# Column sums of w_out by sixteen column-tiled TensorE products in place of GpSimd additions

## The chip, the cores and the metric

The kernel runs on one core of a Trainium2 chip. A core has TensorE (PE in the profile, with its weight loads PEld), VectorE (DVE), ScalarE (ACT), GpSimd (POOL) and SyncE (SP), a working memory SBUF and an accumulation memory PSUM that TensorE writes. The metric is the device time of one execution in microseconds (us).

## What is computed

A block-sorted attention followed by a two-layer network on its output. With B, H, S, D = 4, 8, 768, 64 and eight blocks of 96 rows:

```python
# P: sort_net after five rounds of exp, row and column normalisation (8x8 per head)
k_sorted = einsum('bhij,bhjcd->bhicd', P, k_blocks)
v_sorted = einsum('bhij,bhjcd->bhicd', P, v_blocks)
attn = softmax(scale * q_block @ k_sorted_block.T) @ v_sorted_block
x = attn.transpose(0, 2, 1, 3).reshape(3072, 512)
r = maximum(x @ w_in, 0)          # w_in 512 x 2048
out = (s * r * r + b) @ w_out     # w_out 2048 x 512, s and b scalars
```

The kernel uses that (s r² + b) @ w_out is s (r² @ w_out) plus b times the column sums of w_out. The column sums are one row of 512 numbers, needed once.

## The kernel before

The 3072 tokens are worked on in eight half batches t = 0 to 7 of 384 tokens (four blocks of 96). t // 2 is the batch. For each half batch s_piece (L358) makes scores of a pair of heads and ScalarE's exponential (L361), p_piece (L385 to L390) multiplies by the sorted values and normalises into X[t], and t_piece (L413, for t = 0 and 1) turns X[t] on TensorE into tr and copies it to XT[t] (xt, L228). Later half batches are turned by DMA (x_turn).

ffn1(t) is the first layer: eight steps, each of eight products hps (L442) for 256 of the 2048 inner columns, a Relu on ScalarE (rt, L446), a square on VectorE (gt, L447), and then a call of slot(), which lets one piece of other work into the engines' queues. A Queue spreads its list of pieces evenly over the slots. ffn2(t) is the second layer: three groups of 128 tokens, each sixteen products ops (L468) over the inner columns, with a slot after every four.

The order of work on every engine is the order in which the program is written. Around the change it is: ffn1(0) in two halves (192 tokens each), whose slots hold attention pieces and, in the second half, V1(0) to V1(3) and the turning of half batch 1; then V1(4) and V1(5); then ffn1(1); then ffn2(0) and ffn2(1) with the queue qu, which begins with pieces of batch 1's queries and keys.

V1(i) is v_piece1 (L312 and after): two products tv (L319) of 64 columns of the array each, 512 wide, a cast vn (L228) on VectorE, and two writes dv (L325) to DRAM on SP's queue. When all six are written, v_read(1) on SP's queue (L344) reads the values of batch 1 back in another order; p_piece(2, ...) is the first to use them. build_pd2 (L526) makes the block matrix pd2 for batches 2 and 3, used first by v_piece2 (V2, L333).

The column sums csum are made on GpSimd: after a small copy (gate, L582), which waits for the last piece of X[1], csums(0, 8) adds the first eight of the sixteen 128x512 pieces of w_out (wo_at, tiles wo, loaded at L154) element by element and csums(8, NF) the rest, so csum holds 128 rows of partial sums. bias_piece (L510), in the sixth piece of qu, multiplies by onesf, a 128x128 matrix of ones, which adds up the 128 rows and spreads the sum over all of them, and then by b. GpSimd's queue also issues the loads of q, k, v and the weights: load_v(*brows(3)) stands between the two halves of the additions, load_k for batches 2 and 3 and load_q(2) behind the second, ahead of bias_piece in the same piece.

PSUM tiles come from two pools, psa (three buffers) and psb (two); a new tile of a pool waits until the one whose buffer it takes has been read. tv, ops and pe (of build_pd2) are in psb; hps, tr of a whole half batch and the key pieces of sixteen products are in psa.

Of the kernel before, what the change touches and what calls it, by code (L numbers as in the profile page):

```python
# [9 lines left out]
FP = mybir.dt.float32  # L10
BF = mybir.dt.bfloat16
AF = mybir.ActivationFunctionType
ALU = mybir.AluOpType
# [5 lines left out]
def kernel(  # L19
# [12 lines left out]
    nc = tc.nc  # L32
# [6 lines left out]
    d_model = H * D  # L39
    d_ff = moe_w_in.shape[1]  # L40
    NF = d_ff // 128
    HB = NB // 2
# [10 lines left out]
    const = ctx.enter_context(tc.tile_pool(name="const", bufs=1))  # L53
    sk = ctx.enter_context(tc.tile_pool(name="sk", bufs=1))
# [12 lines left out]
    psb = ctx.enter_context(tc.tile_pool(name="psb", bufs=2, space=bass.MemoryType.PSUM))  # L67
# [22 lines left out]
    def load_v(rows, prow):  # L90
        nc.gpsimd.dma_start(out=vb[prow, 0:BLK, :], in_=vraw[rows])

    def brows(b):
        return slice(b * 64, (b + 1) * 64), slice((b % 2) * 64, (b % 2) * 64 + 64)
# [12 lines left out]
    def new_vs(b):  # L107
        VS[b] = vsp.tile([BLK, 64, VW], BF, tag="vs", name=f"vs{b}")
        nc.vector.memset(VS[b][:, :, D:VW], 1.0)
# [33 lines left out]
    for c0 in range(0, d_ff, FCH):  # L143
        w = const.tile([128, NHP, FCH], BF, name=f"wi{c0}")
        nc.gpsimd.dma_start(
            out=w, in_=moe_w_in.rearrange("(hp p) f -> p hp f", p=128)[:, :, c0:c0 + FCH])
        wis.append(w)
    onesf = const.tile([128, 128], FP)
    nc.gpsimd.memset(onesf, 1.0)

    load_v(*brows(1))
    for f0 in range(0, NF, FW):
        w = const.tile([128, FW, d_model], BF, name=f"wo{f0}")
        nc.gpsimd.dma_start(  # L154
            out=w, in_=moe_w_out.rearrange("(f p) n -> p f n", p=128)[:, f0:f0 + FW, :])
# [4 lines left out]
    def wi_at(hp, f):  # L160
        return wis[f * 128 // FCH][:, hp, f * 128 % FCH:f * 128 % FCH + 128]

    def wo_at(f):
        return wos[f // FW][:, f % FW, :]
# [9 lines left out]
    def zero_pad(r0):  # L174
# [8 lines left out]
                            op=ALU.subtract)  # L183
    between = [lambda: zero_pad(BLK), lambda: zero_pad(BLK + 16), lambda: None,
               lambda: None, lambda: None]
    for it in range(5):
# [5 lines left out]
                                op=ALU.mult)  # L192
# [119 lines left out]
    def v_piece1(c0, eng):  # L312

        pr = brows(1)[1]
        ps = psb.tile([128, 8, D], FP, tag="b", name="tv")
        lhsT = pd1[pr].rearrange("p e m i -> p (e m i)")
        hb = BLK // 2
        for hf in range(2):
            nc.tensor.matmul(out=ps[hf * 64:(hf + 1) * 64], lhsT=lhsT,  # L319
                             rhs=vb[pr, hf * hb + c0:hf * hb + c0 + 8, :],  # L320
                             start=True, stop=True)
        vn = vnp.tile([128, 16, D], BF, tag="vn", name="vn")
        evac(vn[:, 0:8, :], ps, eng)
        for hf in range(2):
            nc.sync.dma_start(out=dv[1][:, hf * hb + c0:hf * hb + c0 + 8, :],  # L325
                              in_=vn[hf * 64:(hf + 1) * 64, 0:8, :])
# [12 lines left out]
    def v_read(b, eng):  # L339
        if b > 1:  # L340
            new_vs(b)
        src = dv[1] if b == 1 else dv[2][(b - 2) * 64:(b - 1) * 64]
        for cp in range(2):
            eng.dma_start(out=VS[b][cp * (BLK // 2):(cp + 1) * (BLK // 2), :, 0:D],  # L344
                          in_=src.rearrange("g (c two) d -> two c g d", two=2)[cp])

    XT, AT, X = {}, {}, {}

    def s_piece(t, hp):

        b, half = divmod(t, 2)
        g0 = (b % 2) * 32 + hp * NB + half * HB
        sc = psa.tile([BLK, 2, 512], FP, tag="a", name="sc")
        for n in range(HB):
            for e in range(2):
                pr = slice(e * 64, (e + 1) * 64)
                q0 = (half * HB + n) * BLK
                nc.tensor.matmul(out=sc[:, e, n * BLK:(n + 1) * BLK], lhsT=ks[pr, g0 + n, :],  # L358
                                 rhs=QT[b][pr, hp, q0:q0 + BLK], start=True, stop=True)
        at = atp.tile([BLK, 2, TG], BF, tag="at", name="at")  # L360
        nc.scalar.activation(out=at, in_=sc[:, :, 0:TG], func=AF.Exp, scale=scale)  # L361
        AT[t, hp] = at

    def p_piece(t, hp, n0=0, nn=HB):

        b, half = divmod(t, 2)
        at = AT[t, hp]
        if t not in X:
            X[t] = xp.tile([BLK, HB, d_model], BF, tag="x", name="x")
        x = X[t]  # L370
        atf = at.rearrange("p e t -> p (e t)")
        if nn < HB:
            p1 = psb.tile([128, 512], FP, tag="b", name="pv")
            pv = [p1[:, e * nn * VW:(e + 1) * nn * VW] for e in range(2)]
            pvv = p1[0:BLK, 0:2 * nn * VW].rearrange("p (e n w) -> p e n w", e=2, w=VW)
        else:
            p2 = psa.tile([128, 2, 512], FP, tag="a", name="pv")
            pv = [p2[:, 0], p2[:, 1]]
            pvv = p2[0:BLK, :, 0:nn * VW].rearrange("p e (n w) -> p e n w", w=VW)
        for e in range(2):  # L380
            for n in range(n0, n0 + nn):
                c0 = (e * HB + n) * BLK
                m = 128 if c0 + 128 <= 2 * TG else BLK
                gi = e * 32 + hp * NB + half * HB + n
                nc.tensor.matmul(out=pv[e][0:m, (n - n0) * VW:(n - n0 + 1) * VW],  # L385
                                 lhsT=atf[:, c0:c0 + m],
                                 rhs=VS[b][:, gi, :], start=True, stop=True)
        rec = rtp.tile([BLK, 2, HB], FP, tag="rec", name="rec")
        nc.vector.reciprocal(out=rec[:, :, 0:nn], in_=pvv[:, :, :, D])  # L389
        nc.vector.tensor_tensor(  # L390
            out=x[:, n0:n0 + nn, hp * 128:(hp + 1) * 128].rearrange("p n (e d) -> p e n d", e=2),
            in0=pvv[:, :, :, 0:D],
            in1=rec[:, :, 0:nn].unsqueeze(3).broadcast_to([BLK, 2, nn, D]), op=ALU.mult)
# [29 lines left out]
    def xt_at(t, hp, n0, nn):  # L423
        if t < 2:
            return XT[t][:, hp, n0 * BLK:(n0 + nn) * BLK]
        return XT[t].rearrange("p (n a) t -> p a n t", a=NHP)[:, hp, n0:n0 + nn, :]
# [6 lines left out]
    def ffn1(t, slot=nothing, n0=0, nn=HB):  # L433
        if t not in GT:
            GT[t] = gtp.tile([128, NF, TG], BF, tag="gt", name="gt")
        gt = GT[t]
        c0, nt = n0 * BLK, nn * BLK
        for f0 in range(0, NF, 2):
            hps = psa.tile([128, 2, 512], FP, tag="a", name="hps")
            for f in range(2):  # L440
                for hp in range(NHP):
                    nc.tensor.matmul(out=hps[:, f, 0:nt], lhsT=wi_at(hp, f0 + f),  # L442
                                     rhs=xt_at(t, hp, n0, nn),
                                     start=(hp == 0), stop=(hp == NHP - 1))
            rt = rtp.tile([128, 2, TG], BF, tag="rt", name="rt")
            nc.scalar.activation(out=rt[:, :, 0:nt], in_=hps[:, :, 0:nt], func=AF.Relu)  # L446
            nc.vector.tensor_tensor(out=gt[:, f0:f0 + 2, c0:c0 + nt], in0=rt[:, :, 0:nt],  # L447
                                    in1=rt[:, :, 0:nt], op=ALU.mult)
            slot()
# [113 lines left out]
    def P(t, hp, *r):  # L563
        return lambda: p_piece(t, hp, *r)

    def SC(t, hp):
        return lambda: s_piece(t, hp)

    def V1(i):
        return lambda: v_piece1(i * 8, "v")  # L570

    ffn1(0, Queue([P(0, 0, 2, 2), P(0, 1, 2, 2), P(0, 2, 2, 2), P(0, 3, 2, 2), SC(1, 2),
                   lambda: t_piece(0, "v", 2, 2), SC(1, 3), P(1, 0)], 8), 0, 2)
    ffn1(0, Queue([V1(0), P(1, 1), V1(1), P(1, 2), V1(2), P(1, 3), V1(3),
                   lambda: t_piece(1, "v")], 8), 2, 2)
    V1(4)()
    V1(5)()


    csum = const.tile([128, d_model], FP)  # L580
    gate = sk.tile([1, 1], BF)
    nc.gpsimd.tensor_copy(out=gate, in_=X[1][0:1, HB - 1, d_model - 1:d_model])  # L582

    def csums(f0, f1):
        for f in range(f0, f1):
            if f == 1:
                nc.gpsimd.tensor_tensor(out=csum, in0=wo_at(0), in1=wo_at(1), op=ALU.add)
            elif f > 1:
                nc.gpsimd.tensor_tensor(out=csum, in0=csum, in1=wo_at(f), op=ALU.add)  # L589

    csums(0, 8)
    v_read(1, nc.sync)
    ffn1(1, Queue([nothing] * 4 + [build_pd2] + [nothing] * 3, 8))
    load_v(*brows(3))
    csums(8, NF)

    V2 = [lambda c0=c0: v_piece2(c0, "s") for c0 in range(0, BLK, 16)]
    qu = Queue([lambda: q_piece(1, 0, "s"), lambda: q_piece(1, 2, "v")]
# [67 lines left out]
```

The softmax here doesn't subtract the row's maximum and nothing guards it: scores larger than these inputs give would overflow.

## Time and profile before

| | |
|---|---|
| median of six runs | 242.44 us (241.93 to 243.02) |
| the profiled execution | 242.49 us |
| its span | 240.8 us |
| GpSimd busy, share of span | 39.3 us, 16% |
| of it the additions (L587, L589) | 15 instructions, 47.7 to 67.9 us |
| VectorE busy from 40 to 50 us | 9.80 of 10 us |
| clock granted to TensorE from 40 us on | 1.00 |

The span runs from the first to the last recorded instruction. Times below are in us from its start. Rows of the timeline give the start, the length, the engine, the line, the operation, what it writes and reads, its shape, and how many instructions the row stands for; a bracket is the idle time of the engine before it and what ended it. Rows of the chain of waits give start, length, engine and line. Lengths of products include the time until their modelled end, so consecutive ones overlap; their rate is read from the starts.

### The profile page before, as it was taken

The page shows a single profiled execution, that of the slowest core. Times are in us where ns is not written, and L with a number is a line of the kernel's source. Part 1 is how long each engine was busy: PE and PEld are TensorE (multiplying, and loading weights), DVE is VectorE, ACT ScalarE, POOL GpSimd, SP SyncE. Part 2 cuts the span into 40 slices and gives each one's busy share as a digit, 9 for nine tenths or more (in the row PEclk, how much of TensorE's full clock was granted, in tenths as well). Part 3 has the DMA queues.
Part 4 walks back from the last instruction along what each step waited for, and adds up shares of the span by engine and source line. Part 5 has one row for each costly group of instructions (what it writes and reads, how often), then busy time and mean ns, then how long its engine had stood idle before and what let it go on. Part 6 is the DMA issues. An engine that isn't in the chain of part 4 may idle for free.

```text
span 240.8 us, 4882 instructions
## 1 busy us (share of the span) xinstructions
PE 227.6 (95%) x2059; PEld 136.2 (57%) x2080; DVE 134.1 (56%) x268; ACT 108.0 (45%) x154; POOL 39.3 (16%) x52
## 2 busy tenths in 40 slices
PE   8978799989999999999998999999999999999993
PEld 4568698845544556555554555666454556654441
DVE  5766557967993558766465647344352544442221
ACT  6347456425438451677626240656522225660000
POOL 7820000199950000450000000000000000000000
PEclk9955579999999999999999999999999999999999
DMA  4999999985999994599902051400014242001212
GB/s 59 182 196 213 223 197 206 224 215 108 136 151 175 278 300 108 129 112 93 158 14 87 9 146 46 109 0 3 1 58 120 64 113 43 0 0 46 83 48 87
DMA packets 29622, 27.33 MB, mean 114 GB/s; under 512 B 16928, under 2 KB 23840, under 8 KB 29088
## 3 DMA queue, kind: packets, MB, share of 16 engines
q0 software_dynamic: 8400, 15.21, 38.4%
q1 hardware_dynamic: 21200, 11.81, 21.2%
q8 instruction: 16, 0.26, 0.5%
q14 instruction: 6, 0.05, 0.1%
HBM read 29.63 MB, written 8.65 MB: 159 GB/s over the span
## 4 chain that ended last, share of the span: by engine, by line
PE 83%; DVE 7%; DMA 6%; issue 2%; POOL 1%; ACT 1%; POOLq 0%
PE hps L442 34%; PE ops L468 33%; DMA vb<-in_v_dram 6%; PE sc L358 3%; PE pv L385 3%; PE tv L303 3%; PE tk L277 2%; PE tq L259 2%; DVE x L390 2%; DVE ks L228 1%; PE tv L333 1%; DVE gt L447 1%; DVE vn L228 1%; DVE ot L459 1%; PE tq L244 1%
## 5 line engine op out<-in xcount | busy, mean ns | idle before, releaser
L442 PE MATMUL hps<-xt,wi 128*128 128x384 bf16 (+1 forms) x576 | 89.0, 311 | 1.0 <-DVE xt L228 1.0
L468 PE MATMUL ops<-wo,gt 128*128 128x512 bf16 x363 | 87.7, 379 | 1.5 <-issue 0.5
L446 ACT ACTIVATE rt<-hps 128x768 bf16<-128x768 f32 (+1 forms) x72 | 53.3, 740 | 52.8 <-PE hps L442 51.7
L442 PEld LDWEIGHTS <-wi 128*128 128x128 bf16 x576 | 54.1, 99 | 31.2 <-issue 2.3
L447 DVE TENSOR_TENSOR gt<-rt 128x768 bf16<-128x768 bf16 (+1 forms) x72 | 42.0, 586 | 41.4 <-ACT rt L446 41.0
L468 PEld LDWEIGHTS <-gt 128*128 128x128 bf16 x384 | 35.0, 98 | 38.4 <-issue 0.6
L361 ACT ACTIVATE at<-sc 96x768 bf16<-96x768 f32 x32 | 24.3, 802 | 35.1 <-PE sc L358 35.1
L459 DVE SCALAR_TENSOR_TENSOR ot<-ops,s_bc,bias 128x512 f32<-128x512 f32 x24 | 18.0, 749 | 38.0 <-PE ops L468 37.8
L228 DVE CAST ks<-tk 64x512 bf16<-64x512 f32 (+1 forms) x36 | 20.9, 579 | 4.6 <-PE tk L277 4.1
L390 DVE TENSOR_TENSOR x<-pv,rec 96x512 bf16<-96x512 f32 (+1 forms) x36 | 22.6, 628 | 1.3
L589 POOL TENSOR_TENSOR csum<-csum,wo 128x512 f32<-128x512 f32 x14 | 17.6, 1255 | 1.0
L230 ACT CAST ks<-tk 64x256 bf16<-64x256 f32 (+1 forms) x28 | 13.7, 490 | 8.7 <-PE tk L277 8.4
L385 PEld LDWEIGHTS <-at 96*128 96x128 bf16 (+1 forms) x256 | 11.9, 104 | 4.1 <-ACT qt L230 1.0
L385 PE MATMUL pv<-vs,at 96*128 96x66 bf16 (+1 forms) x256 | 12.9, 199 | 0.8 <-DVE rec L389 0.6
L358 PEld LDWEIGHTS <-ks 64*96 64x96 bf16 x256 | 8.4, 132 | 6.8 <-issue 5.0
L389 DVE RECIPROCAL rec<-pv 96x8 f32<-96x8 f32 (+1 forms) x36 | 6.9, 192 | 9.2 <-PE pv L385 9.2
L358 PE MATMUL sc<-qt,ks 64*96 64x96 bf16 x256 | 10.7, 223 | 1.0 <-DVE x L390 1.0
L172 PE MATMUL wp<-zt 128*128 128x256 bf16 x50 | 9.5, 318 | 1.1 <-DVE warm L104 1.1
L277 PEld LDWEIGHTS <-kb 64*128 64x128 bf16 x192 | 7.5, 103 | 5.4 <-issue 5.3
L277 PE MATMUL tk<-pd,kb 64*128 64x64 bf16 x192 | 9.0, 202 | 0.9 <-DVE pd L520 0.9
L230 ACT CAST vn<-tv 128x1024 bf16<-128x1024 f32 x6 | 6.1, 1012 | 4.1 <-PE tv L333 2.3
L172 PEld LDWEIGHTS <-zt 128*128 128x128 bf16 x50 | 4.9, 101 | 5.2 <-DVE warm L104 1.1
(67 smaller groups left out, 102.5 us busy)
## 6 DMA issues: line engine op xcount, KB each, us to landing
out_dram<-ot SPq DMA_DIRECT2D x24, 256.0 KB, 2.2
kb<-in_k_dram POOLq DMA_DIRECT2D x4, 768.0 KB, 10.8
vb<-in_v_dram POOLq DMA_DIRECT2D x4, 768.0 KB, 19.0
qr<-in_q_dram POOLq DMA_DIRECT2D x3, 768.0 KB, 20.4
wi<-in_moe_w_in_dram POOLq DMA_DIRECT2D x2, 1024.0 KB, 19.0
wo<-in_moe_w_out_dram POOLq DMA_DIRECT2D x2, 1024.0 KB, 30.1
dv<-vn SPq DMA_DIRECT2D x6, 256.0 KB, 7.8
vs<-dv POOLq DMA_DIRECT2D x4, 384.0 KB, 12.0
```

Source lines behind the costliest of these rows:

```text
L228: nc.vector.tensor_copy(out=out, in_=in_)
L230: nc.scalar.copy(out=out, in_=in_)
L277: nc.tensor.matmul(out=ps[:, c, :], lhsT=kb[pr, c0 + 2 * c:c0 + 2 * c + 2, :].rearrange("p c d -> p (c d)"), rhs=rhs, start=True, stop=True)
L358: nc.tensor.matmul(out=sc[:, e, n * BLK:(n + 1) * BLK], lhsT=ks[pr, g0 + n, :], rhs=QT[b][pr, hp, q0:q0 + BLK], start=True, stop=True)
L361: nc.scalar.activation(out=at, in_=sc[:, :, 0:TG], func=AF.Exp, scale=scale)
L385: nc.tensor.matmul(out=pv[e][0:m, (n - n0) * VW:(n - n0 + 1) * VW], lhsT=atf[:, c0:c0 + m], rhs=VS[b][:, gi, :], start=True, stop=True)
L390: nc.vector.tensor_tensor(out=x[:, n0:n0 + nn, hp * 128:(hp + 1) * 128].rearrange("p n (e d) -> p e n d", e=2), in0=pvv[:, :, :, 0:D], in1 ...
L442: nc.tensor.matmul(out=hps[:, f, 0:nt], lhsT=wi_at(hp, f0 + f), rhs=xt_at(t, hp, n0, nn), start=(hp == 0), stop=(hp == NHP - 1))
L446: nc.scalar.activation(out=rt[:, :, 0:nt], in_=hps[:, :, 0:nt], func=AF.Relu)
L447: nc.vector.tensor_tensor(out=gt[:, f0:f0 + 2, c0:c0 + nt], in0=rt[:, :, 0:nt], in1=rt[:, :, 0:nt], op=ALU.mult)
L459: nc.vector.scalar_tensor_tensor(out=ot, in0=ops, scalar=s_bc, in1=bias, op0=ALU.mult, op1=ALU.add)
L468: nc.tensor.matmul(out=ops, lhsT=gt[:, f, m * 128:(m + 1) * 128], rhs=wo_at(f), start=(f == 0), stop=(f == NF - 1))
```

## The change

The GpSimd additions and their gate go. A new csums() on TensorE takes their place, called once between ffn1(0) and ffn1(1): sixteen products with a 128x32 matrix of ones, each summing the 128 rows of one piece of w_out into 32 equal rows of a PSUM tile cs. Piece f goes to rows 32 (f mod 4) onward, so four groups of 32 columns of the array take turns and each accumulates four pieces. ScalarE copies cs to csum. Since every sum now stands in 32 equal rows, onesf becomes 1/32. V1(4), V1(5) and v_read(1) move from between the layers into the first three slots of ffn1(1), and build_pd2 from the fifth slot to the seventh. load_v(*brows(3)) stays behind ffn1(1) in the text, with no additions ahead of it or behind it on GpSimd's queue.

```diff
     onesf = const.tile([128, 128], FP)
-    nc.gpsimd.memset(onesf, 1.0)
+    nc.gpsimd.memset(onesf, 1.0 / 32)
+    ones = const.tile([128, 32], BF)
+    nc.gpsimd.memset(ones, 1.0)
...
+    csum = const.tile([128, d_model], FP)
+
+    def csums():
+
+        cs = psb.tile([128, d_model], FP, tag="b", name="cs")
+        for f in range(NF):
+            g = f % 4
+            nc.tensor.matmul(out=cs[g * 32:(g + 1) * 32], lhsT=ones[:, 0:32], rhs=wo_at(f),
+                             start=(f < 4), stop=(f >= NF - 4))
+        nc.scalar.copy(out=csum, in_=cs)
+
     ffn1(0, Queue([P(0, 0, 2, 2), P(0, 1, 2, 2), P(0, 2, 2, 2), P(0, 3, 2, 2), SC(1, 2),
                    lambda: t_piece(0, "v", 2, 2), SC(1, 3), P(1, 0)], 8), 0, 2)
     ffn1(0, Queue([V1(0), P(1, 1), V1(1), P(1, 2), V1(2), P(1, 3), V1(3),
                    lambda: t_piece(1, "v")], 8), 2, 2)
-    V1(4)()
-    V1(5)()
-
-
-    csum = const.tile([128, d_model], FP)
-    gate = sk.tile([1, 1], BF)
-    nc.gpsimd.tensor_copy(out=gate, in_=X[1][0:1, HB - 1, d_model - 1:d_model])
-
-    def csums(f0, f1):
-        for f in range(f0, f1):
-            if f == 1:
-                nc.gpsimd.tensor_tensor(out=csum, in0=wo_at(0), in1=wo_at(1), op=ALU.add)
-            elif f > 1:
-                nc.gpsimd.tensor_tensor(out=csum, in0=csum, in1=wo_at(f), op=ALU.add)
-
-    csums(0, 8)
-    v_read(1, nc.sync)
-    ffn1(1, Queue([nothing] * 4 + [build_pd2] + [nothing] * 3, 8))
+    csums()
+
+    ffn1(1, Queue([V1(4), V1(5), lambda: v_read(1, nc.sync)] + [nothing] * 3 + [build_pd2, nothing], 8))
     load_v(*brows(3))
-    csums(8, NF)
```

## The prediction

> **What bounds the kernel now.** I read the busy shares first, then the chain of waits, then the timeline around the change.
>
> ```profile
> PE 227.6 (95%) x2059; PEld 136.2 (57%) x2080; DVE 134.1 (56%) x268; ACT 108.0 (45%) x154; POOL 39.3 (16%) x52
> PE 83%; DVE 7%; DMA 6%; issue 2%; POOL 1%; ACT 1%; POOLq 0%
> ```
>
> TensorE is busy 95% of the span and is 83% of the chain; GpSimd, whose additions go away, is 1%, none of it from the column sums. So the 18.7 us of additions (14 of 1.255 and one of 1.14) are not for sale. What counts is what they do to others, and what TensorE must now do. The place is between the two first layers, in the chain of waits:
>
> ```profile
> 47.65 0.60 DVE vn L228
> 48.25 0.77 DVE gt L447
> 49.02 0.88 DVE xt L228
> 49.94 6.66 PE hps L442 x40
> 56.60 0.36 PE pe L213 x2
> 56.96 4.01 PE hps L442 x24
> ...
> 80.07 0.54 PE pv L385 x16
> ```
>
> Here TensorE waits for VectorE: ffn1(1) cannot start before the copy xt (L228) of half batch 1. Afterwards the chain is TensorE alone, 64 hps products at 0.166 us. The timeline (start, length) of the same place:
>
> ```profile
> 47.49 0.85 PE L413 MATMUL tr<-ident,x 96*128 96x96 bf16 x16
> 47.66 1.14 POOL L587 TENSOR_TENSOR csum<-wo 128x512 f32<-128x512 bf16 x1
> 48.22 0.80 DVE L447 TENSOR_TENSOR gt<-rt 128x384 bf16<-128x384 bf16 x1
> 48.27 0.14 PEld L319 LDWEIGHTS <-pd 64*64 64x64 bf16 x4
> 48.51 0.38 PE L319 MATMUL tv<-vb,pd 64*64 64x512 bf16 x2
> 48.82 0.10 PEld L442 LDWEIGHTS <-wi 128*128 128x128 bf16 x1 [0.41 <-issue]
> 48.94 0.94 DVE L228 COPY xt<-tr 128x1536 bf16<-128x1536 bf16 x1
> 49.94 6.66 PE L442 MATMUL hps<-xt,wi 128*128 128x384 bf16 x40 [1.05 <-DVE xt L228]
> ```
>
> Between the transposes tr and 49.94 TensorE does V1(4) and V1(5) (tv, from 48.27) and then idles 1.05 us. The change puts the column sums into this hole and takes V1(4), V1(5) out.
>
> **The xt copy comes sooner: -0.45.** The gt before it took 0.80 beside the first addition; the same shape without one takes 0.34 to 0.36 and releases the next instruction 0.27 after its start (37.93 to 38.20, before the earlier xt). So xt starts at 48.22 + 0.27 = 48.49, after the last tr (48.34). Its 0.94 fits the half-size copy (0.553 for 768 columns) without a stretch, so I keep it: it ends at 49.43, and hps can start 0.06 later, as now: 49.49 instead of 49.94. If gt stays at 0.80 the gain is nothing.
>
> **Sixteen column-sum products: nothing, if they run four at a time.** No row shows a product on 32 columns of the array. The nearest is tv: two 64-column products, each 512 wide, both start at 48.27, the next two at 48.51. So two products on different columns share 0.24 us, and from the last start to the next weight load of hps are 0.31 us (48.51 to 48.82). Bounds: four at a time, last start 48.27 + 3 x 0.24 = 48.99, free at 49.30, hidden under xt (49.49) with 0.19 to spare. One after the other at the 0.216 of a full product (ops, 0.86 for four): last start 48.27 + 15 x 0.216 = 51.51, free at 51.82, that is 1.88 past 49.94. In between, two at a time: 48.27 + 7 x 0.24 + 0.31 = 50.26, 0.32 past. I take four, by the tv row, the only one with column tiles. The cover is xt; without it they cost 1.03 us.
>
> A rule of the Trainium skill speaks against this: "TensorE: Matmul & The Clock Gate", Part 3, (packing small matmuls), says a weight load overlaps running products only where its row group differs, and all sixteen use all rows. By it each load would wait for the product before: an estimate of 16 x (0.10 + 0.38) = 7.7 us with the rows' load and product lengths, ending near 56 and making the kernel about 6.8 us slower. The row above disagrees: four tv loads of one row group lie within 0.14 us while the first pair runs until 48.67. The same Part gives 2.38 times for three column tiles, by which I estimate the sixteen at 16 x 0.216 / 2.38 = 1.45 us and the start of hps at about 49.9; no run here shows it.
>
> **V1(4) and V1(5) move into ffn1(1): +0.82.** They were free in the hole; now they stand between hps products, where TensorE has no gap (the 40 hps above are back to back). The same insertion exists in the second half of ffn1(0):
>
> ```profile
> 41.67 0.83 PE L442 MATMUL hps<-xt,wi 128*128 128x192 bf16 x8
> 42.43 0.40 PE L319 MATMUL tv<-vb,pd 64*64 64x512 bf16 x2
> 42.76 0.83 PE L442 MATMUL hps<-xt,wi 128*128 128x192 bf16 x8
> 43.43 0.43 PE L385 MATMUL pv<-vs,at 96*128 96x66 bf16 x8
> ```
>
> From hps to hps around tv are 1.09 us, and eight hps without it take 0.67 (42.76 to 43.43): 0.42 for a V1. The 64-row key pieces in ffn1(2) cost 0.41 (2.71 + 0.34 around 16 hps, which alone take 16 x 0.165 = 2.64). I take 0.41 each, 0.82 together; bounds 0.33 (products alone) and 0.45. build_pd2 moves from the fifth to the seventh slot at the same price. Its result pd2 is needed at 73.3 and would be ready near 61.
>
> **What costs nothing, and under what cover.** The copy of cs by ScalarE: nearest rows 0.58 (64x512) and 1.01 (128x1024), so about 0.6 from 49.4; ScalarE is idle from 48.18 to 51.43 now. cs takes a psb buffer; the next to want it is V1(5) at about 49.49 + 2 x 1.32 + 0.41 = 52.5. V1's two casts (0.68 each) go to a VectorE that has 0.7 of every 1.3 us free in ffn1(1) once gt is back at its 0.56. Gt itself (1.16 beside the additions, 0.56 later) is faster, but TensorE never waited for it there. The memset of ones: about 0.2 us on POOL at 8.9, ahead of load_v(1), w_out, q1 and k1. TensorE now needs w_out at 48.27; it lands 28.0 and 32.1 us after its issues at 9.4 and 10.3, so by 42.4.
>
> **The queues.** POOL's gate and additions go, so load_v(3) is held only by V1(5)'s reading and is issued near 53 (now 56.74), and load_k(2) right behind it near 53.5 (now 67.83). load_k(3) still waits for the last key piece (69.3), with load_q(2) behind it. On SP, v_read stays behind the twelve dv writes. V1(5)'s cast ends near 54.6, its writes go out by about 56, as now. But they then share the engines with two loads: such writes landed in 2.2 us late and 8.6 to 10.4 us under load. So v_read issues between 58.3 and 64.5 (now 58.32); it flies 10.4 to 14 us, thus lands by 78.5 at worst. Its first reader is pv at 80.07. Cover: 1.6 us at the worst end, 6 at the best; behind it on SP are the out writes from 73.4, which it would not reach.
>
> **Sum.** -0.45 + 0 + 0.82 = +0.37 us: the profiled span 240.8 becomes 241.2 and its execution 242.49 becomes 242.86. The median is 242.44, so 242.8. That is 0.15%, inside the 0.2% that a measurement of this kernel can tell from no change. Bounds of this case: -0.45 + 0.66 = +0.2 to 0 + 0.9 = +0.9, or 242.6 to 243.3.
>
> **Rivals.**
> 1. Two at a time. For: no row shows more than two. Against: nothing in the tv row says two is the most. 0.32 + 0.82 = +1.14: 243.6.
> 2. One after the other. The place is the hole at 48.3; it decides as soon as the sixteen take more than 1.2 us, each further microsecond a full one. 1.88 + 0.82 = +2.70: 245.1. Against: the tv pairs.
> 3. The read of the batch-1 values comes late at P2(2,0). It decides from a landing at 80.4 on. If it is issued at 64.5 and takes 2 us more than the longest such flight (15.8), it lands at 82.3: +0.37 + 1.9, 244.7. Against: the loads it would share with are then nearly over.
> 4. Faster. VectorE is relieved, and that is worth more than one gt: the chain has a stretch on VectorE's key casts (69.7 to 71.9) where TensorE waits about 0.28. If that went and V1 were hidden, -0.45 - 0.28 = -0.73: 241.7. Against: those casts start with TensorE's own key products, after the last addition (67.9), and no addition touches them.
>
> That the sums are not moved at all is not a case; the additions leave the program.
>
> **How the numbers follow.** Likeliest 0.62 (0.41 within 0.2%, 0.21 above), two at a time 0.11, serial 0.07, late read 0.06, faster 0.14 (0.12 beyond 0.2%, 0.02 within). So faster 0.12, same 0.41 + 0.02 = 0.43, slower 0.21 + 0.11 + 0.07 + 0.06 = 0.45. The time is that of the likeliest, 242.8. The range runs from 242.1 to 245.2: it takes in the serial bound and leaves out most of the faster case and half of the late one, some 0.15.
>
> **What would show it.** hps of ffn1(1) starts near 49.5 with xt as its releaser (csums hidden); if the releaser is the sums, rivals 1 or 2. Starts of the sums in groups of four 0.24 apart. gt before xt at 0.36. hps to hps around V1 0.41 more than without. load_k(2) issued near 53.5. pv of P2(2,0) without a wait for vs. I am wrong if the sixteen take over 1.2 us, or if a V1 costs less than 0.25.

## The result

| | before | after |
|---|---|---|
| median | 242.44 us (49 executions, 241.59 to 243.20) | 243.48 us (24 executions, 242.49 to 244.10) |
| ratio to before | | 1.0039, 95% interval 1.0029 to 1.0048 |
| the profiled execution | 242.49 | 243.31 |
| its span | 240.8 | 241.2 |
| the rest of its time, outside the span | 1.7 | 2.1 |

The changed kernel is slower by 0.39%, about 0.95 us. The profiled executions differ by 0.82 us, half of it (0.46) inside the span and half (0.4) outside it. Ratios leave out executions more than 1.5% above the fastest of their kernel; there were two, both in experiment 6.

The chain and the busy times of the changed kernel's page:

```profile
PE 229.0 (95%) x2075; PEld 136.6 (57%) x2096; DVE 128.6 (53%) x268; ACT 108.5 (45%) x155; POOL 20.5 (9%) x37
PE 84%; DVE 6%; DMA 6%; issue 2%; POOL 1%; ACT 1%; POOLq 0%
```

GpSimd lost 18.8 us of work and VectorE, which was slowed by it, 5.5. TensorE, the bound, gained 1.4. The timeline of the changed kernel between the layers (start, length, as before):

```profile
47.52 0.84 PE L415 MATMUL tr<-ident,x 96*128 96x96 bf16 x16
48.24 0.36 DVE L449 TENSOR_TENSOR gt<-rt 128x384 bf16<-128x384 bf16 x1
48.30 0.55 PEld L581 LDWEIGHTS <-ones 128*32 128x32 bf16 x16
48.30 1.05 PE L581 MATMUL cs<-wo,ones 128*32 128x512 bf16 x16
48.52 0.95 DVE L230 COPY xt<-tr 128x1536 bf16<-128x1536 bf16 x1
49.40 0.59 ACT L583 COPY csum<-cs 128x512 f32<-128x512 f32 x1 [1.18 <-PE cs L581]
49.52 1.46 PE L444 MATMUL hps<-xt,wi 128*128 128x384 bf16 x8 [0.18 <-DVE xt L230]
50.91 0.40 PE L321 MATMUL tv<-vb,pd 64*64 64x512 bf16 x2
51.25 1.47 PE L444 MATMUL hps<-xt,wi 128*128 128x384 bf16 x8
52.65 0.40 PE L321 MATMUL tv<-vb,pd 64*64 64x512 bf16 x2
52.99 6.67 PE L444 MATMUL hps<-xt,wi 128*128 128x384 bf16 x40
```

The reader is to see three things. gt is back at 0.36, so xt and with it hps come 0.42 sooner (49.52, was 49.94; tr, ahead of both, began 0.03 later than before). The sixteen sums fit under xt: hps waits for xt, 0.18, and not for them. And between starts of hps around each V1 stand 1.73 and 1.74 us; eight hps alone take 1.30, so a V1 costs 0.44. The first ops start at 61.27, 0.47 later than before, and nothing further on changes that: the span grew by 0.46.

Executions differ by up to 1.5 us in when tr begins: in the profiles used here at 46.6 to 47.4 where the mean granted clock is 0.964 or 0.965, and at 47.5 to 48.2 where it is lower. The low clock lies ahead of 40 us (before: 0.82 up to 20 us, 0.66 from there to 40, then 1.00). So stages are compared below from the start of tr: hps starts at tr + 2.44 before and tr + 2.00 after; the span ends at tr + 193.27 and tr + 193.69.

### The profile page after: what moved, and what is told of

Its sections match the earlier page's. It is cut to its first block, busy times and chain, and to the rows that moved or that the text cites. A ratio compares the mean times of both kernels' runs of the same rounds, so it can differ in the third digit from the quotient of the medians.

```text
span 241.2 us, 4899 instructions
## 1 busy us (share of the span) xinstructions
PE 229.0 (95%) x2075; PEld 136.6 (57%) x2096; DVE 128.6 (53%) x268; ACT 108.5 (45%) x155; POOL 20.5 (9%) x37
## 3 DMA queue, kind: packets, MB, share of 16 engines
q1 hardware_dynamic: 21200, 11.81, 21.1%
## 4 chain that ended last, share of the span: by engine, by line
PE 84%; DVE 6%; DMA 6%; issue 2%; POOL 1%; ACT 1%; POOLq 0%
PE hps L444 34%; PE ops L470 34%; DMA vb<-in_v_dram 6%; PE sc L360 3%; PE pv L387 3%; PE tv L305 2%; PE tk L279 2%; PE tq L261 2%; DVE x L392 2%; PE tv L335 1%; DVE gt L449 1%; DVE vn L230 1%; DVE ot L461 1%; PE tq L246 1%; DVE ks L230 1%
## 5 line engine op out<-in xcount | busy, mean ns | idle before, releaser
L449 DVE TENSOR_TENSOR gt<-rt 128x768 bf16<-128x768 bf16 (+1 forms) x72 | 36.9, 513 | 45.8 <-ACT rt L448 45.4
L230 DVE COPY qt<-tq 128x1536 bf16<-128x1536 bf16 x4 | 7.0, 1758 | 3.0 <-PE tq L261 3.0
## 6 DMA issues: line engine op xcount, KB each, us to landing
kb<-in_k_dram POOLq DMA_DIRECT2D x4, 768.0 KB, 10.4
wi<-in_moe_w_in_dram POOLq DMA_DIRECT2D x2, 1024.0 KB, 18.8
vs<-dv POOLq DMA_DIRECT2D x4, 384.0 KB, 11.4
```

Of the source, the lines that this page charges most:

```text
L230: nc.vector.tensor_copy(out=out, in_=in_)
```

## Experiments

**1. V1(4) and V1(5) back between the layers, behind the sums.**

```diff
     csums()
-    ffn1(1, Queue([V1(4), V1(5), lambda: v_read(1, nc.sync)] + [nothing] * 3 + [build_pd2, nothing], 8))
+    V1(4)()
+    V1(5)()
+    v_read(1, nc.sync)
+    ffn1(1, Queue([nothing] * 4 + [build_pd2] + [nothing] * 3, 8))
```

> The changed kernel with V1(4) and V1(5) put back between the layers, behind the sixteen sums. Theory (the slots of ffn1(1) cost 0.44 us for each V1, the gap is nearly free): the sums are through at 49.3, the four tv products take 0.5 to 0.6, hps starts at 49.85 to 49.95 and the first ops near 60.75, that is 0.4 to 0.5 before the changed kernel; span 240.7 to 240.9. Rival (the 0.46 that the span grew come from elsewhere, from loads that now start earlier or from ScalarE's copy): the span stays at 241.2. Time: outside the span the changed kernel has 2.1 us and the kernel before 1.7; if this goes with the 32 added TensorE instructions or with the shorter GpSimd program, it is 2.1 here and the time about 242.9.

Measured: ratio 1.0024 (1.0008 to 1.0040), hps at tr + 2.85, span end at tr + 193.65. The timeline of this kernel shows why almost nothing was gained:

```profile
47.67 1.05 PE L581 MATMUL cs<-wo,ones 128*32 128x512 bf16 x16
48.65 0.40 PE L321 MATMUL tv<-vb,pd 64*64 64x512 bf16 x2
49.41 0.40 PE L321 MATMUL tv<-vb,pd 64*64 64x512 bf16 x2 [0.35 <-ACT csum L583]
```

V1(5) takes the buffer of cs and waits for ScalarE's copy. With two psb buffers, the order sums, V1, V1 brings that copy onto the path. The expectation missed this; experiment 7 takes the wait out.

**2. The moved pieces alone, additions left on GpSimd.**

```diff
-    V1(4)()
-    V1(5)()
...
-    v_read(1, nc.sync)
-    ffn1(1, Queue([nothing] * 4 + [build_pd2] + [nothing] * 3, 8))
+    ffn1(1, Queue([V1(4), V1(5), lambda: v_read(1, nc.sync)] + [nothing] * 3 + [build_pd2, nothing], 8))
```

> The kernel before with only V1(4), V1(5), v_read(1) and build_pd2 moved into the slots of ffn1(1), the additions left on GpSimd. Theory: hps still starts at 49.94, since gt beside the first addition still takes 0.8; the two V1 cost 0.89, first ops at 61.7, span 241.7, 0.9 over the kernel before. Rival (a V1 in a slot is cheap and the growth comes from the sums): span 240.8 to 241.1. Outside the span: 1.7 if it goes with TensorE's instruction count or with GpSimd's program, 2.1 if it goes with the moved pieces; time about 243.3 by theory.

Measured: ratio 1.0048 (1.0028 to 1.0067), hps at tr + 2.44, first ops 0.88 later than in the kernel before (from tr), span end at tr + 194.26, that is 0.99 over it; 1.70 outside. The theory holds: the two V1 cost 0.88 by themselves, and the sums, which the changed kernel has and this one has not, cost nothing. The last 0.11 come further on, where the chain of this kernel runs over VectorE, which now has two more casts beside the additions:

```profile
57.72 5.90 DVE gt L447 x4
```

**3. The additions kept, their gate set behind the last gt of ffn1(0).**

```diff
-    nc.gpsimd.tensor_copy(out=gate, in_=X[1][0:1, HB - 1, d_model - 1:d_model])
+    nc.gpsimd.tensor_copy(out=gate, in_=GT[0][0:1, NF - 1, TG - 1:TG])
```

> The kernel before with the gate of the GpSimd additions behind the last square gt of ffn1(0) instead of the last piece of X[1]; nothing else changes. Theory: the gt before xt goes back to 0.36, hps starts at 49.5, everything after is 0.42 earlier, span 240.4, time 242.0; the additions end near 68.8, still ahead of the bias product (69.4). Rival (the first addition does not set gt's 0.8, or the later end of the additions delays the bias product): span 240.8 or above. Outside the span 1.7 by both theories on it.

Measured: ratio 0.9995 (0.9979 to 1.0012); hps at tr + 2.00 as expected, so gt's 0.80 was the first addition's doing. But the span ends at tr + 193.9. In its timeline TensorE stands still further on, before the queries of batch 2, whose load has only just landed:

```profile
88.40 1.04 PE L468 MATMUL ops<-wo,gt 128*128 128x512 bf16 x4
90.31 0.86 PE L259 MATMUL tq<-ident,qr 128*64 128x128 bf16 x24 [0.87 <-DMA qr<-in_q_dram]
```

The load of q was issued 0.7 sooner (69.1, before 69.8) but flew 21.1 us instead of 20.4, so it landed at 90.2 as before. In the kernel before, tq came at 90.57. But in this execution tr itself began 0.87 sooner (46.62, before 47.49), so the wait of 0.87 met a TensorE that was 1.3 ahead, and not only the 0.44 from xt. How long tq waits in an execution with a later tr was not profiled; the times of all twelve show no gain.

**4. No column sums at all.**

```diff
-    gate = sk.tile([1, 1], BF)
-    nc.gpsimd.tensor_copy(out=gate, in_=X[1][0:1, HB - 1, d_model - 1:d_model])
+    nc.gpsimd.memset(csum, 0.0)
...
-    csums(0, 8)
...
-    csums(8, NF)
```

> The kernel before without the column sums: csum is set to zero once, so the b term is left out of the output; V1(4) and V1(5) stay between the layers. Theory: the additions' whole price is the 0.42 at xt, hps at 49.5, span 240.4, the same as with the later gate. Rival (the additions cost more, through VectorE in ffn1(1) or through the loads queued behind them): span clearly below 240.4. Outside the span: 1.7 if it goes with TensorE's instruction count, 2.1 if it goes with GpSimd's shorter program.

Measured: ratio 0.9994 (0.9979 to 1.0008); hps at tr + 2.00, span end at tr + 192.8, 0.46 below the kernel before: inside the span the theory is right. The time shows none of it because 2.09 us, not 1.7, lie outside. VectorE's rows of this kernel and of the kernel before show a second effect of the additions:

```profile
61.41 0.56 DVE L447 TENSOR_TENSOR gt<-rt 128x768 bf16<-128x768 bf16 x1 [0.74 <-ACT rt L446]
63.98 1.76 DVE L228 COPY qt<-tq 128x1536 bf16<-128x1536 bf16 x1 [2.02 <-PE tq L259]
```

```profile
60.04 4.37 DVE L447 TENSOR_TENSOR gt<-rt 128x768 bf16<-128x768 bf16 x3
64.42 1.76 DVE L228 COPY qt<-tq 128x1536 bf16<-128x1536 bf16 x1
```

Without additions (first fence) VectorE waits 2.02 us for TensorE before qt. Beside them (second fence, before) three gt take 4.37 instead of 1.7 and qt starts with no wait at all: here VectorE had no time left, though nothing in the chain of the kernel before said so.

**5. The later gate, with load_k(2) sent ahead of the second half of the additions.**

```diff
     load_v(*brows(3))
+    load_k(*brows(2))
     csums(8, NF)
...
-               + [seq(lambda: load_k(*brows(2)), lambda: load_k(*brows(3)), lambda: load_q(2), bias_piece), ...
+               + [seq(lambda: load_k(*brows(3)), lambda: load_q(2), bias_piece), ...
```

> The kernel with the later gate, and load_k(2) taken out of the bias piece and put on GpSimd's queue ahead of the second half of the additions. Theory (the later gate gains 0.42 at xt, and lost it where tq of batch 2 waited for the load of q): load_k(2) moves its bytes before load_q(2) is issued, the load of q lands sooner, tq waits for nothing, and the kernel is 0.45 faster than the kernel before in the span, 1.7 outside; time 242.0. Rival (the gain at xt is lost somewhere else too, or the load of q lands no sooner): tq still waits up to 1 us, time 242.4.

Measured: ratio 1.0016 (0.9993 to 1.0039), span end at tr + 193.5. The wait for q is gone, as expected, but the time did not follow. The waits of this kernel's weight loads and products after 58 us (waiter, released by, us, times, longest):

```profile
PEld bps L512 <- POOL csum L589: 0.6, 1, 0.6
```

```profile
PE sc L358 <- DVE ks L228: 0.3, 1, 0.3
```

Now the additions are late for the bias product, and VectorE for the keys. The theory falls: with the additions in the program TensorE met a wait at three places when it came sooner (0.87 for q in experiment 3, 0.6 for the bias product and 0.3 for the keys here).

**6. The changed kernel with fifteen one-element GpSimd memsets at the end of its queue.**

```diff
     load_q(3)
+    pad = sk.tile([1, 1], FP)
+    for _ in range(15):
+        nc.gpsimd.memset(pad, 0.0)
```

> The changed kernel with fifteen GpSimd memsets of one element behind its last load (near 106 us), as many instructions as the additions that it dropped. They hide behind TensorE: span as the changed kernel, 241.4. Theory (the 0.4 us outside the span go with the number of instructions in GpSimd's program): 1.7 outside, time 243.05. Rival (they go with the additions themselves, or with what GpSimd does early): 2.1 outside, time 243.5.

Measured: ratio 1.0015 (0.9998 to 1.0031), median 243.01; 1.69 outside, so the 0.4 go with the length of GpSimd's program. Two of its twelve executions were 4 to 5 us longer, and the profile is of one of them (span 246.7); it shows the late read of rival 3. From its chain:

```profile
55.21 10.27 DMA dv<-vn
...
66.02 18.11 DMA vs<-dv
84.13 0.05 issue
84.17 0.71 PE pv L387 x16
```

The last write of V1(5) lands at 65.5, the read issued at 66.0 lands at 84.13, and pv waits 3.7 us for it. In the same profile the clock granted from 84 to 88 us is 0.60, where the changed kernel has 1.00, so the late read came with more than its own wait. Whether the memsets have a part in that is not shown; they come at about 106 us, long after, but see experiment 9.

**7. Experiment 1 with the sums' tile in psa.**

```diff
-        cs = psb.tile([128, d_model], FP, tag="b", name="cs")
+        cs = psa.tile([128, 2, 512], FP, tag="a", name="cs")[:, 0]
```

> V1(4) and V1(5) behind the sums as in the earlier trial, but the sums' PSUM tile taken from psa, so that V1(5) does not wait for ScalarE's copy (it waited 0.35 and hps started 2.07 after the first sum instead of 1.6). Theory (each V1 in a slot costs 0.44): hps 1.55 to 1.65 after the first sum, against 1.22 in the changed kernel, and nothing between hps; span 0.5 below the changed kernel (240.9 at the same clock), outside 2.1, time 243.0. Rival (something else in ffn1(1) grew): no more than 0.1 below the changed kernel.

Measured: ratio 1.0015 (0.9996 to 1.0034), median 243.01; hps 1.53 after the first sum, span end at tr + 193.11, 0.58 below the changed kernel and 0.15 below the kernel before; 2.10 outside. The theory holds.

**8. All sixteen sums on the same 32 columns.**

```diff
     csum = const.tile([128, d_model], FP)
+    nc.gpsimd.memset(csum, 0.0)
...
-            g = f % 4
-            nc.tensor.matmul(out=cs[g * 32:(g + 1) * 32], lhsT=ones[:, 0:32], rhs=wo_at(f),
-                             start=(f < 4), stop=(f >= NF - 4))
-        nc.scalar.copy(out=csum, in_=cs)
+            nc.tensor.matmul(out=cs[0:32], lhsT=ones[:, 0:32], rhs=wo_at(f),
+                             start=(f == 0), stop=(f == NF - 1))
+        nc.scalar.copy(out=csum[0:32], in_=cs[0:32])
```

> The changed kernel with all sixteen sums on the same 32 columns of the array, the other 96 rows of csum set to zero once; the output is the same. Theory (the sums are cheap because four run at once): starts 0.216 apart, the last one 3.24 after the first, hps 3.5 to 3.6 after the first sum instead of 1.22, span 2.3 above the changed kernel, 243.7, time 245.8. Rival (the products are cheap for having only 32 columns of weights): no change.

Measured: ratio 1.0126 (1.0095 to 1.0157), median 245.62, hps at tr + 4.33, 2.33 later than in the changed kernel, as expected. The sums' own rows (length min/median/max in ns, first and last start), first of this kernel, then of the changed one:

```profile
L581 PE MATMUL cs<-wo,ones x16: 379/379/389, 48.5 to 51.7; 128*32 128x512 bf16 x16
```

```profile
L581 PE MATMUL cs<-wo,ones x16: 379/379/389, 48.3 to 49.0; 128*32 128x512 bf16 x16
```

Each product has the same length. On one column group they start one by one, 0.22 us apart (48.48 to 51.73 in fifteen steps). On four groups they start four at a time, each four within 0.01 us, at 48.30, 48.52, 48.74 and 48.95: four products take the 0.22 of one. In the chains of this kernel and of experiment 1 the sixteen hold TensorE 3.56 and 1.01 us, up to the start of what follows: 3.5 times as fast.

**9. Number 7 with the fifteen memsets.** The edits are those of 1, 7 and 6.

> The sums in a psa tile, V1(4) and V1(5) behind them between the layers, and fifteen one-element GpSimd memsets behind the last load. Theory: span as in the trial without the memsets (240.9, 0.1 below the kernel before at the same clock), outside 1.7 instead of 2.1, time 242.5, not slower than the kernel before and 0.9 below the changed kernel. Rival (the memsets did not set the 1.7 of the padded changed kernel): 2.1 outside, 243.0.

Measured: ratio 1.0002 (0.9982 to 1.0021), median 242.58 against 242.72 for the kernel before beside it; 1.70 outside. It takes back what the change lost, and does not measurably beat the kernel before. Two of its twelve executions lie 1.4 and 1.7 us above its median. With the two of experiment 6 that makes four of the 24 with fifteen memsets behind the changed sums; of the 48 of the changed kernel and experiments 1 and 7, which have none, no execution lies more than 0.7 above its median. Whether the memsets cause this stays open.

**10 to 12. The time outside the span against the number of GpSimd instructions.** One execution each of the changed kernel with five and with thirty memsets and of the kernel before with fifteen (the edit of 6 with other counts).

> The changed kernel with five memsets instead of fifteen. If the time outside the span falls evenly with GpSimd's instructions (0.41 for fifteen): 1.97. If it falls in a step: 2.1 or 1.7. Span as the changed kernel.

> The kernel before with fifteen memsets behind the last load. Even fall: 1.3 outside. A step already passed: 1.7. Span as the kernel before.

> The changed kernel with thirty memsets. Even fall: 1.3 outside; a step passed with fifteen: 1.7, as in the kernel before with fifteen. Span as the changed kernel.

The three gave 2.04, 1.72 and 1.70. All kernels together (GpSimd's instructions from the page's first part, packets of the queue of kind q14 instruction from its third, median time outside the span):

| kernels | GpSimd instructions | q14 packets | outside, us |
|---|---|---|---|
| after; experiments 1, 4, 7 | 37 | 5 | 2.11; 2.11, 2.09, 2.10 |
| experiment 8 | 38 | 5 | 2.03 |
| after with five memsets | 42 | 5 | 2.04 |
| before (76 executions); experiments 2, 3, 5, 6, 9 | 52 | 6 | 1.71; 1.70, 1.70, 1.70, 1.69, 1.70 |
| after with thirty, before with fifteen memsets | 67 | 6 | 1.70, 1.72 |

Most of it is a step between 42 and 52 instructions: an even fall would have given 1.3 at 67. It goes with one packet of instructions more in the span; which of the two counts sets it is not shown. The rows at 38 and 42 instructions lie 0.05 to 0.08 below those at 37, and that at 42 is one execution. TensorE's count has no part in it: it is the same in before and experiment 4. Whether the 0.4 lie ahead of the first recorded instruction or behind the last, and why a shorter program should have more, stays open.

## Why the prediction was right or wrong

**Inside the span it was right, term by term.** The xt copy was put at -0.45: measured 2.00 - 2.44 = -0.44 from tr, and experiments 3 and 4 show that the first addition was the cause. The sums were put at nothing under the cover of xt, free at 49.30, with 0.19 to spare: TensorE waited 0.18 for xt after them. V1 was put at 0.41 each and cost 0.44. The sum was +0.37, the profiled spans differ by 0.46, and by 0.43 from tr. Experiment 2 shows the V1 term alone (0.88 at the first ops).

**Outside the span it was not: the step is "the profiled span 240.8 becomes 241.2 and its execution 242.49 becomes 242.86".** The span did become 241.2; the execution became 243.31. The prediction took the 1.7 us around the span as given, a change of nothing for which it gave no reason. They became 2.1 because GpSimd's program lost its additions: without them and without the sums they are 2.09 (experiment 4), and with as many memsets at the queue's end 1.69 and 1.70 (experiments 6 and 9). With that the time left the likeliest case's own range (242.6 to 243.3) by 0.2 and went from within 0.2% to 0.39% slower. That it stayed in the whole range, 242.1 to 245.2, is luck: the upper end stood there for sums that run one after the other, and they did not.

**Rivals 1 and 2.** Four at a time was right, in groups 0.22 apart where the tv row had given 0.24. The serial price is real: 4.33 - 2.44 = 1.89 past the old start of hps in experiment 8, where 1.88 was worked out. The rule cited against the change from the Trainium skill ("TensorE: Matmul & The Clock Gate", Part 3: a weight load overlaps running products only where its row group differs) does not hold here: sixteen loads of one row group lie within 0.55 us beside the products. By its 2.38 times for three column tiles the prediction had estimated hps at about 49.9; it came at 49.52, and the four column groups ran 3.5 times as fast as one.

**Rival 3** did not set the time of the changed kernel, but its mechanism exists. The prediction gave 58.3 to 64.5 for the issue of v_read; SP's row of the changed kernel has 65.10, past its end:

```profile
65.10 2.57 SPq L346 DMA_DIRECT2D vs<-dv  x2
```

and the two loads went ahead as foreseen, on GpSimd's queue:

```profile
53.36 0.52 POOL L91 DMA_DIRECT2D vb<-in_v_dram  x1 [28.70 <-PE tv L321]
53.87 0.52 POOL L88 DMA_DIRECT2D kb<-in_k_dram  x1
```

So the cover for pv is some 7 us thinner in issue than before, and one profiled execution of experiment 6 fell through it (landing 84.13, wait 3.7). The upper end of the flight was mis-sized: the rival allowed 2 us over the 15.8 of before, and flights of 18.1 (experiment 6) and 20.2 (experiment 5) occurred. Nor do the prediction's 6 us of cover "at the best" follow from its own figures: 80.07 less 58.3 and a flight of 10.4 to 14 leaves 7.8 to 11.4.

**Rival 4** did not happen: even without any additions (experiment 4) the span falls by 0.46, the xt term alone. But the reason given against it was incomplete. It said that no addition touches the key casts. In experiments 3 and 5, where TensorE comes sooner, they do: VectorE has no pause from the slowed gt over qt to the eight ks, and TensorE waits 0.2 and 0.3 for keys.

## What to carry to other kernels

Work that sits in a wait is free, and moving it to make room for other work gives it its full price: here two V1 went from nothing to 0.9 us, twice what the relieved copy gained. A gain upstream has to be followed past every buffer, queue and load that was just in time before; experiments 1, 3 and 5 each met one. Compare spans as well as times: here half of the difference came with a program's length on an engine that is off the critical path, and no row inside the span will show it.

## What the runs showed of the hardware

- Four column groups of the array, 128x32 each, run 512-wide products four at a time, and sixteen of them 3.5 times as fast as one group (1.01 against 3.56 us). The first weight load of the full-width products follows 0.31 us after the last of them starts (48.96 to 49.27 in the changed kernel).
- A VectorE product of two bf16 tiles in SBUF takes 0.36 alone and 0.80 beside a GpSimd addition (128x384), 0.56 alone and up to 1.51 beside it (128x768). A copy from PSUM is not slowed (xt 0.94 beside an addition, 0.95 without).
- The time outside the span has a step of 0.3 to 0.4 us, at a GpSimd program somewhere between 42 and 52 recorded instructions: the shorter program has more (2.03 to 2.11, against 1.69 to 1.72).
